# Another order of an attention's instructions, and 91 instead of 58 of its sums on VectorE

## The chip, the core and the metric

The kernel runs on one core of one Trainium2 chip. Its time is the device time of one execution in microseconds (us). In the trace PE is TensorE's matmuls and PEld its weight loads, DVE is VectorE, ACT ScalarE, POOL GpSimd, SP SyncE, which issues most of the DMAs. SBUF is the on-chip memory that all engines share, PSUM the smaller one that matmuls write.

## The reference, cut to what matters

```python
# attention: 4 batches x 8 heads, 1152 keys of 64, queries pooled in pairs (576 of them)
q_pool = q.reshape(B, H, S // 2, 2, D).mean(axis=3)
scores = scale * np.matmul(q_pool, k.transpose(0, 1, 3, 2))
scores = scores - np.max(scores, axis=-1, keepdims=True)
attn = np.exp(scores)
attn = attn / (np.sum(attn, axis=-1, keepdims=True) + 1e-09)
x = np.matmul(attn, v)            # -> 2304 rows x 512
# then a soft mixture of 8 experts (w1, w2) on x, dispatched by softmax over rows of x @ phi,
# and combined by softmax over slots; then
h = x @ w_in
out = (h * np.cos(h)) @ w_out
```

All of it is float32. The weights w_in and w_out are converted inside the kernel, during the attention, into another number format (clamp, shift, sign, round) and stored to DRAM for the last stage.

## The kernel before

The attention works on pairs of heads, p = 0 to 15, and each pair has two halves of the queries, a = 0 and 1, of 288 each. For each half there are nine key tiles, t = 0 to 8, of 128 keys. Per (p, a, t): `scores` (L453) writes a 128 x 576 tile of PSUM with eight matmuls, among them one that subtracts the row maximum; `exps` (L468) on ScalarE takes the exponential into an SBUF tile E, of which there are five; `av` (L493) multiplies by v on TensorE; and `e_sum` (L477) adds E to the running sum ES, also in SBUF. For t = 1 the sum is ES = E0 + E1 (L486), from t = 2 on ES = ES + E (L488), so the sums of one half are a chain. `on_vector` (L474) says whether a sum runs on VectorE or on GpSimd: the table VEC (L48) has one string for each half, and a sum is on VectorE if its t is among the digits.

Before the scores of a pair, `prep` (L880) makes its operands: `sum_q` (L344) adds neighbouring queries (VectorE, SBUF to SBUF), `tr_q` and `tr_k` transpose on TensorE, `q_hi`/`k_hi` and `q_lo`/`k_lo` split the results into two parts on ScalarE and VectorE, and 15 `max_pair` (matmuls, L410) with 15 `max_pair_red` (L420, a maximum on VectorE from PSUM into the tile nm) find the row maxima. These maxima of pair p+1 are spread among the scores of pair p. `fin` (L926) turns the sums into reciprocals and normalises the pair; after every fourth pair it also computes that batch's share of the mixture's dispatch (`b_logits`, which reads phi, and what follows).

`convert(i)` (L959), i = 0 to 31, turns one piece of w_in or w_out: load, two ScalarE steps (`conv_act`, `conv_low`), three VectorE steps in SBUF (`conv_clamp` L296, `conv_shift` L302, `conv_sign` L308), a GpSimd addition (`conv_round` L314) and a store. Conversions are spread over the attention too.

Each of these is an `Op` that `add()` puts on a list, 2,500 in all, with what it depends on. `in_order` (L118) then issues them in the order that ORDER (L54) writes out: two characters are one index into the list, in base 64 by DIGITS. Each engine works through its own instructions in that order and waits by semaphores for what they need; nothing else ties the engines' times to each other. An Op with `take="2"` uses one of four PSUM slots, one with `take="E"` one of the five E tiles; each takes the slot that has been free longest in the list.

SyncE issues the loads and stores in the order of the same list, each of them waiting for its buffer: q, k and v, the conversions, phi, the first 40 pieces of the experts' weights into a ring (`ring_piece`, 256 KB each) and further pieces (`late_piece`) into buffers that the attention has done with. After the attention the mixture's experts consume these pieces while the ring loads the rest; the last stage (cosine and two matrix products) follows.

Of the kernel before, what the change touches and what calls it, by code (L numbers as in the profile page):

```python
# [52 lines left out]
)  # L53
ORDER = (  # L54
    "0102XrXs0304050H0809XuXvXw06070L0M0P240Q0B0C0R0SXtXx0F0G0J220N0K0I0O0D0W0E0T0A0U0V0X0Y230Z28290l0m2B0o0pXy0s000t"
    "0w0x0+0a250-0bXz262C46470q272D0c0d2A0n0r0u0y100v0z1112X+2E0g0h13140e0f0iY017181B1F1C2L2M15191D2F161AY11G1E1IY22G"
# [2 lines left out]
    "2j3037382e2f2m3B3C3F3G6B4N4O2n2o3J3K4VYDYCYEYF4W4XYGYH34393D3H3L3A3E4Y3I3M1y1z3O3N4R3P4S3R3S3V3W4e3Z3d4f3aYI1+4P"
    "4QYL3T3X4T3Q4U3U3Y3c3e3g4Z1-3h4L4a3i3j3m3nYJYK4M3b3f3q3r3u4k483v4b6E4c3l3p4l3t3k3o3s3x8Y6F4d4t6I3w3yYM4g4wbsbtYN"  # L60
    "204u4+4h4x214i4-4jYOYP4yYQYRYS525356576G6H6K6L3z4v4z506M51556C6J8b3+3-595A4o4p5B545F5C6T5G6U5J5K5N4m4n4q6N6O405E"
    "5O5I5M5QYT4r5R584s6V6W6R5D8Z5H5LAc415S5T5V5Z6S5W5a6b6c5d5e5h5P6d5i6e6Z6a5U5Y42YUYWYXYY5X5bYb5c5fYVYZ43Ya5g5k5l6P"
    "6Q6X5m5q5u5n5y6Y6f5r5j5o5s5v5w5z6k6lbu8e8cAf8d8g8f6g6hYc8h5p5t5x5-6m8i8j606x6+6n6yYe5+8k72766-7073776q6r7A7B4445"
    "616263YfYg748p8q6s6tbr6oYdbvYjYh6z787175796pYi7D6i7E7F6j7G8l7J6u7K7N7R8m7C7H7L7O7P8z8+7S8x8yYk7I7M64YmYnYoCg6v6w"
    "7Q7UAd657VYl66YpYq7W7X8-907Z7a7dYr7e8r8s7h7i7l8v8w6798997Ybw7c7b7m7g7k7o7p8n7f8o7q7r7j7n8t8u918a7u7v7y807z819697"
    "9495YsYuYt7s7w7+Ag92937t7x7-839J9M849QAhAk9K9U9N68Yv9A7T9R9VYw82859Y699BAiAmAe869OYxYz879Z9S9CCjAnAoAjAl9L9P9T9X"
    "9Wbx9D9b9c9E9d9F9e9h9iAr9G9l9p8889As9m9a8A8BAt9fAu9q9H9I9g9kYybyY+Z0Y-9o9s9t9u9jAz9n9vA+9x9-9y9zZ1A0AxAyA3A7A1Z2"
    "8CA4B1Ek9w9+A28D8IA8B2Z58JAvAwA6AAZ3Z4AB8MA-8NACB0ADAGApAHbz8K8LAqAKAOA5A9ALB3AEB4AP9rZ6B5Z8Z9Z78O8PChAI8E8F8GCk"
    "EnB6B7AMAQAFAJANZAARZBZDClCoAS8S8T8HBABBBNBOb+BQBRBSBCBDZCBUBVBYB8BZB9BcBd8Q8RCmBWBaBeBIBJCnATCp8UAUAV8VBPBTBXb-"
    "c0BbBfBgZEBGBHBhBlBEBiBmBjZGBpBqBFBKAWAXAYCzC+8WBLBM8XCiBtZHZICxCyc1BnBrBuCtBkBoZFZLCuZJAZBsBwBxZKCqCrByB-C3BvBz"  # L70
    "CsC0C4C-D0C7C8D5D6CBCGH9CCD3D1ZMB+D2ZNC2C6CAc2C1D4CHCECFElZOZPCvCwCKC5C9c3CDCICLCMD7D8D9COCSZQZTZREoCPCQEpDAEsCT"
    "CJCNCRCVCWDBDEDFZSDRDSDCDDDUDVDYDcDZDdDGDHCUDgDhAaAbCXCYCZEqErDWEuEmDKEvHCDLEwDTDXDbc4Etc5ZUZVDfDjDkZWEzE+DlDmDM"
    "DNDpDtDaDqZXDxDuc6CaCbDIZYF3DoDsDJDODwDeDiDnDrCcDPDyD+ZZZaDQE0DvDzF4D-F1CdE3E1ZbE7F2c7E4ExE8EBEFEyECF9FAE-E2E5E9"
    "E6EAEGF7FBF0F8F5ZcEDEEEIF6EJEKHAEOESEHELc8CeFCFDEPJDEMEQETc9CfEUEWEXFIZeHDZfZgZjFEZdHEENFFEREVEZFJHHFGEaFHFVFWFO"
    "FPEYFYFcFZFdFgFhFKFLFkFlFpHFHJHGJGHIFXHKHLFbZhZiZkZlZmcAcBFfFjFnEbFaFeFiFqFoEcZnEdFtFuZoHMFxF-HNFQZpZqFyFMFmFrFs"
    "FRG0FNFSFvFzFwF+G2G3FTHQFUHWHRG4G5HXG7G8cCG9GBGCHUHVGFGGGJZrHYEeHZEfGDHBHOHPJEZsZuG6GAGEZvZwGKGIGMGNGHHcGOZtZxHd"
    "HaGPHbEgGSGWGaGLGTGQHSGXZyHhGbGRGVHTEhcDJHHeHfHgGUHiGZGdGeHwHlJIJLHzHxZzI1G1cEHmH+GYGcI2I5I6HpI9HqEiIAJJEjJNLHJO"
    "JPZ+Z-GfGga0a1JKH-cFa2HyI0I4GhJMI8ICIDHjHkIEIFHnHoIIIJLIIMIQI3I7cGIBJYINJZHrHsHtIHILIRIPITa3GiIUGjHuHvIGJSJWIVGk"
    "GlJTIKIOISIYIcIWJQJXIZIaIdJRIgIeIkIhJUJVJgIiIlImIXIbIfJcJhLKJea5GmGnIjInIoJfJdGoGpa4a6GrJaGqJbIpIqItIuJiIxIyJnJo"
    "I-J0cHGwGxIrJlJmGyGzLLcIJja8JkIvLMLNLOGsGta9a7aALPIsIwcJLQI+NLcKJFJ2J3H0H1GuGvIzJ+J-JpJ1JqK1K5K2LRK6LSLULVJ4J5K9"  # L80
    "LTaDJtJ6KAKDKIaBaCK3JuKEaEK7JvJwLYK0K4LZK8KCaGaHKJaFKGKHNMG+G-aILaLbKMKNKQH2LWKRLXJ7J8KBcLKUaLKFH3JrH5H7JsJxJyH4"
    "KVJzaJKKKOKSaKJ9H6JAH8aMaNKLKPKTNOKXKYKWaOKZKcKaLkaPKdLlKgKhKkKoKeKlLeLfLiLjKbKfKjKnKiKmPmLJKpKrKsKqKtaQKuLgKxLh"
    "KyK-L0LcKvLdLmL3NRL4aRJBJCKzL1NPNSLnNQLoNTKwK+L2NUL6L7LtLuM2M5M3cMM6LpLqaTcNM9MAL5M7NYL8NZL9aSLzMDMHL+aUaWMENVNW"
    "LxaXaYLANXMIM4M8MCMGLyMKaVMLLvMBPpLwMMLrMQMUMNLsMFMJaZLBMRMOMSMVMYNmNeNfcOcPMZMWMPMTMXL-M0M1RqMbNnMcNgNhMdMgMeMh"
    "NcMaaaMiNdLCMkMoMlMpNoNpMsLDMxMtNiNjabacadaeafNaNbMfMjMnLEMrMyMvMwNkNlMmMqM-N0NtNuN3N4PnN7PsNqN8agNvNrNwMuMzN1M+"
    "N2N6NAPtPvahNBNxNsO6NyO7NNLFLGO9OAO1O2ODcQOHaiOENzN5N9NCOIN+NDPwPxajPycRNEOLOMN-O0PqO3PrO8OCPuOGRrOBOFOJakOKOOam"
    "anaoOPRtO4O5OQOUalORP-OVcSONQ0OYOZOcOdPzP+NFarOSapNGNHNIQ5OWQ6OTOXOaObOfOgOhQ1OiOkOoQ2OlQ3aqOpOsOeOwQ4Q9cTQ7OtQA"
    "asauavOjOnawOrOvOxOzO+QBO-atNJQ8QCOmOqP0OuP3TuNKQDPoP7P4QEQFP8PBaxPCazQIQJRwOyRuP1RxRzRvRyQGQHP5P9P2P6PAPEPFaya+"
    "b0QXQaQeQYQbb1QfQiQjb2PDQQQRQcQmQgQkQnQoPGPHPIR+R-S0QMQKRsQLQZQdQhQNTvQlQpQqS1S2Qra-QsQOQPQvQzQwQtQ+PJPKS5PLS6R1"
    "R2b3PMQSQTSFQuQUb5QyR0SGQVR4TxR5QWR6S3R9RDR7QxQ-R3S4SBRARESCRHRIRLS7S8RMPNPOR8RCRGRKb4b6b7RBROPTRPPUS9RQSDPPb8b9"  # L90
    "bAbBbDRFSASERRPQSHPSPRRJRURYSIRcbCRVRZRNPdSJSKRdSLTyRSRWPVPePWSMSNRTRXRbPfTzRfPZSQbEU0bGRgVySbPgbFbHPaSRPXSeScSW"
    "PYbISfSXRaSiSjSmPbSnSOSPRePiPcT+SgPhU2bLPjU3U4bJbKT-PkPlVzRhRiRjU1SqSrSSSTSUSdbMShSlSpStSuSVSkSYSZSvSaSwSoSsSxbO"
    "UBUCSzS+T1T2U5U6T5T6TATBS-U9UAUDRkUESyT0T4T8bPT9TDTET3ULT7UMTHTwRlTLRmTITMTFTJUFTPUHcfRnbQTCTGTQUGUITKTObNbRV-TS"
    "TTU7TUTNU8UJTVTYTcUKUNTZTdchTgUSThUTUQTRTWW0W1UOUPTXTbW4TaTeTiURTfTjTkUYUZUabTbSbUUfUgUiUmUbUjUqUnUrbWbXUWUXUuUv"
    "RoRpbYW2UUbbTlcUTmUhTnUkUoUsUlW3UpUtUVbVUcUxUyW5UdUeUzU+UwWJWKV1V2V5V6WDV9WEVAVEbZbaU-WBWCW9V0V4VFV8V+ToTpVCWAbc"
    "VDbdWFWGW6W7W8VHV3VLVPVTVIV7cgVMWLWHTqbebfbgVJVNbhbiVQVRVGTrbjVKVOVSWIVUVWWMWPVYVcVXWQVZVdWNWOWRVgVhWaVkTsVbVfVj"
    "WbVVVaVeViVlVmVBbkblVnVockWSWTVpVqVrTtWYWZWjWmWkcnbmWUWnWqWVWrbnWuWvWeWfWyboWzcbX1WoWcWdbpVsVtVuWWWXWgWlX2WpWtWx"
    "W-cVVvWscWWwWhWiW+X3cccdX5X0X9X6XAXDX7XBXEX4X8XFXCXGXIXLXHcpVwXJXMVxcZclXPXTXXXQcmcXXKXOcYcqcoXNXRcjcicaXUXYXVXZ"
# [1430 lines left out]
```

## Time and profile before

| | us |
|---|---|
| median of 3 runs | 802.92 (799.06 to 803.47) |
| the profiled execution | 802.07 |
| its span, first to last instruction | 800.3 |
| attention up to the first scores | 24.05 |
| from there to the last pair's first scores | 460.15 |

The page lists for the whole span: PE busy 739.7 us, DVE 603.8, ACT 448.8, POOL 455.3. A busy PE is not PE at its peak, since matmuls overlap and their ends are modelled. Waits are read with the engine that ended them: "A <- B" means that A sat idle until B's instruction was done. A row with three durations gives the shortest, median and longest of a group.

### The profile page before, as it was taken

Reading aid. Unit: us, or ns where it says so; the run is one execution under the profiler, and the core shown is the slowest. Engines: PE = TensorE matmul, PEld = TensorE weight load, DVE = VectorE, ACT = ScalarE, POOL = GpSimd, SP = SyncE. Lnnn points to the kernel's source line nnn. Section 1 sums busy time; section 2 is a strip of 40 time slices with the busy share of each in tenths; the row PEclk is TensorE's granted clock in tenths of the full one; section 3 lists DMA queues with packets and bytes.
Section 4 is the critical chain, followed back from the end, with each engine's and each line's share of the span. In section 5 each row is a group of like instructions: output and inputs, shape, how many; then the busy total and the mean of one; then the engine's idle time right before and its main releaser. Section 6 shows DMA issues by size and latency. Waiting matters only on the chain.

```text
span 800.3 us, 16402 instructions
## 1 busy us (share of the span) xinstructions
PE 739.7 (92%) x6336; PEld 536.9 (67%) x6336; DVE 603.8 (75%) x902; ACT 448.8 (56%) x838; POOL 455.3 (57%) x373
## 2 busy tenths in 40 slices
...
GB/s 228 74 101 106 188 75 180 128 167 133 141 203 116 231 84 145 121 142 191 118 110 127 41 124 162 236 332 384 386 55 26 28 27 20 8 27 27 27 27 26
DMA packets 86482, 101.48 MB, mean 127 GB/s; under 512 B 48260, under 2 KB 48260, under 8 KB 86404
## 3 DMA queue, kind: packets, MB, share of 16 engines
...
q10 hardware_dynamic: 6020, 0.34, 0.5%
...
q14 instruction: 28, 0.23, 0.1%
...
## 4 chain that ended last, share of the span: by engine, by line
PE 59%; DVE 26%; DMA 6%; issue 4%; ACT 3%; POOL 1%; SPq 0%; DVEq 0%; ACTq 0%; POOLq 0%
PE o L1433 15%; PE mx L460 11%; PE mx L498 9%; DVE nm L424 8%; PE o L1435 8%; PE mx L415 4%; PE mx L463 3%; DVE cvt L304 3%; DVE cvt L310 3%; DVE ES L488 3%; DVE cvt L298 2%; PE h L1229 2%; PE u L1397 2%; DVE qs L347 2%; DMA w<-in_moe_w_dram 1%
## 5 line engine op out<-in xcount | busy, mean ns | idle before, releaser
L488 POOL TENSOR_TENSOR ES<-ES,E 128x576 f32<-128x576 f32 x169 | 246.3, 1459 | 65.2 <-DVE ES L488 35.1
L424 DVE TENSOR_REDUCE nm<-mx 128x2 f32<-128x768 f32 x240 | 222.8, 950 | 38.1 <-PE mx L415 37.0
L471 ACT ACTIVATE E<-mx 128x576 f32<-128x576 f32 x288 | 178.2, 651 | 95.3 <-PE mx L463 80.4
L460 PE MATMUL mx<-Q,kX 64*128 64x288 f32 x1152 | 174.8, 318 | 17.3 <-DVE nm L424 13.7
L498 PE MATMUL mx<-E,vn 128*64 128x288 f32 x1152 | 157.6, 416 | 0.0
L1417 POOL TENSOR_TENSOR lo<-g,hi 128x512 fp32r<-128x512 f32 (+1 forms) x73 | 94.2, 1290 | 110.7 <-DVE hi L1415 105.9
L460 PEld LDWEIGHTS mx<-Q,kX 64*128 64x128 f32 x1152 | 113.1, 192 | 38.4 <-DVE nm L424 20.4
L498 PEld LDWEIGHTS mx<-E,vn 128*64 128x64 f32 x1152 | 76.8, 138 | 57.3 <-ACT E L471 6.8
L1433 PE MATMUL o<-w_hi,hi 128*128 128x512 f32 x288 | 113.1, 393 | 0.7 <-DVE hi L1415 0.7
L1435 PE MATMUL o<-w_lo,hi 128*128 128x512 f32 x288 | 113.2, 393 | 0.3 <-DVE w_lo L1321 0.3
L415 PE MATMUL mx<-kX,Q 64*128 64x384 f32 x480 | 88.3, 389 | 17.3 <-DVE nm L424 9.0
L460 PE MATMUL mx<-Q,kY 64*128 64x288 f32 x576 | 88.1, 300 | 0.0
L463 PE MATMUL mx<-NM,one_row 64*128 64x288 f32 x576 | 87.9, 299 | 0.0
L1433 PE MATMUL o<-w_hi,lo 128*128 128x512 f32 x288 | 77.4, 389 | 0.0
L1404 DVE SCALAR_TENSOR_TENSOR r<-t,u 128x512 f32<-128x512 f32 (+1 forms) x73 | 49.4, 678 | 36.5 <-ACT t L1402 35.9
L1413 DVE SCALAR_TENSOR_TENSOR g<-r,u 128x512 f32<-128x512 f32 (+1 forms) x73 | 49.6, 679 | 35.4 <-ACT r L1411 35.3
L1402 ACT ACTIVATE t<-u 128x512 f32<-128x512 f32 (+1 forms) x73 | 42.9, 591 | 58.2 <-PE u L1397 58.1
L415 PEld LDWEIGHTS mx<-kX,Q 64*128 64x128 f32 x480 | 45.9, 193 | 40.8 <-DVE nm L424 17.5
L316 POOL TENSOR_TENSOR cvt<-cvt 128x512 uint32<-128x512 uint32 x32 | 43.2, 1350 | 40.3 <-ACT cvt L294 14.6
L486 POOL TENSOR_TENSOR ES<-E 128x576 f32<-128x576 f32 x28 | 41.8, 1494 | 40.3 <-ACT E L471 34.7
L1433 PEld LDWEIGHTS o<-w_hi,lo 128*128 128x128 f32 x288 | 54.0, 188 | 11.5
L1433 PEld LDWEIGHTS o<-w_hi,hi 128*128 128x128 f32 x288 | 54.2, 188 | 10.8 <-DVE hi L1415 0.9
...
## 6 DMA issues: line engine op xcount, KB each, us to landing
...
```

The source lines that it names most:

```text
L415: nc.tensor.matmul(out=m[:, h, 0:384], lhsT=Q1[p % 2][hs, AT[i]:AT[i] + 128], rhs=X[p][hs, ks], start=True, stop=True)
L424: nc.vector.tensor_reduce(out=nm3[p][:, i, :, c:c + 1], in_=m[:, :, 0:384], axis=AX.X, op=ALU.max)
L460: nc.tensor.matmul(out=sc[:, h, 0:HF], lhsT=x[hs, ks], rhs=y[hs, qs], start=(n == 0), stop=False)
L463: nc.tensor.matmul(out=sc[:, h, 0:HF], lhsT=one_row[hs, :], rhs=NM[p % 2][hs, qs], start=False, stop=True)
L471: nc.scalar.activation(out=e, in_=sc[:, :, 0:HF], func=AF.Exp, scale=1.0 / 16.0)
L488: eng.tensor_tensor(out=ES[p, a], in0=ES[p, a], in1=E[p, a, t], op=ALU.add)
L498: nc.tensor.matmul(out=av_t[p, a, g][64 * h:64 * h + 64, 0:HF], lhsT=vn[p][:, h, t, :], rhs=E[p, a, t][:, h, :], start=(t == g), stop=(t = ...
L1404: nc.vector.scalar_tensor_tensor(out=r, in0=t, scalar=MAGIC, in1=u, op0=ALU.subtract, op1=ALU.subtract)
L1413: nc.vector.scalar_tensor_tensor(out=g, in0=r, scalar=1.0, in1=u, op0=ALU.subtract, op1=ALU.mult)
L1417: nc.gpsimd.tensor_tensor(out=lo[:, 0:n], in0=g, in1=hi[:, 0:n].bitcast(FP32), op=ALU.subtract)
L1433: nc.tensor.matmul(out=o, lhsT=x, rhs=w_hi[ff], start=(ff == 0 and not part), stop=bool(part and ff == NF - 1))
L1435: nc.tensor.matmul(out=o, lhsT=x, rhs=w_lo[ff], start=False, stop=False)
```

## The change

Two tables are replaced: VEC, whose digits go from 58 to 91, and ORDER, the whole list. With them, the load of phi becomes the first Op of the list instead of one after the conversions (so that all indices shift by one), and `b_logits` names it among what it depends on. No instruction's form changes; 33 additions move from GpSimd to VectorE, and all 2,500 Ops are issued in another order.

```diff
 VEC = (
-    "38", "3", "", "27", "2", "4", "", "7",
-    "4", "5", "28", "", "6", "8", "", "458",
-    "", "68", "78", "136", "", "6", "46", "567",
-    "12", "256", "34", "3", "4", "12678", "2345678", "1234567",
+    "468", "1", "45", "2468", "25", "237", "4", "1267",
+    "36", "6", "6", "12367", "68", "67", "15", "7",
+    "568", "1", "4578", "126", "4", "24568", "4", "2367",
+    "234", "17", "238", "137", "67", "123568", "2345678", "1234567",
 )
 ORDER = (
-    "0102XrXs0304050H0809XuXvXw06070L0M0P240Q0B0C0R0SXtXx0F0G0J220N0K0I0O0D0W0E0T0A0U0V0X0Y230Z28290l0m2B0o0pXy0s000t"
...
+    "020304050709060G080H0A0OXsXt0PXu0Q0R0M0N0E0F0C0D0S0I0J0K0L2429010T2A0U0X0Y0V0b0W0m23250B2C0n0p0t0x0qXvXwXxXyXz26"
...
 )
...
-                bl[b] = m = add(b_logits, b, deps=[mul[p], bp0.get(b - 1), bp1.get(b - 1)], take="2")
+                bl[b] = m = add(b_logits, b, deps=[mul[p], bp0.get(b - 1), bp1.get(b - 1), lp], take="2")
...
+        lp = add(load_phi)
         for p in range(NP):
             prep(p)
             main(p)
...
         for i in range(NU):
             convert(i)
-        add(load_phi)
```

Decoded, the beginning of the list reads before: sum_q(0), tr_q(0), conv_load(0), conv_act(0), q_hi(0), tr_k(0, first part), k_hi, max_pair, tr_k (second part), k_hi, conv_clamp(0), conv_shift(0), conv_sign(0), q_lo(0), k_lo(0), and the maxima. After: sum_q(0), tr_q(0), q_hi(0), tr_k, q_lo(0), tr_k, k_hi, max_pair, k_lo, the first maximum, k_hi, max_pair, conv_load(0), conv_act(0), and more maxima; conv_clamp(0), conv_shift(0) and conv_sign(0) come after the first four scores.

## Rows read from the trace of the kernel before

**Rows 1.** Stretches: length; PE, PEld, DVE, ACT, POOL busy us; clock, DMA share, GB/s.
```profile
24.05:484.20 460.15, 424.87 (x4545) 306.41 (x4543) 407.38 (x533) 272.53 (x504) 329.25 (x240) 0.98 0.47 133
484.20:527.30 43.10, 38.64 (x350) 24.78 (x346) 30.32 (x62) 17.61 (x39) 2.87 (x3) 0.96 0.68 215
527.30:575.60 48.30, 46.59 (x351) 19.09 (x352) 13.80 (x58) 16.82 (x48) 13.85 (x33) 1.00 1.04 382
```

**Rows 2.** Who waited for whom, 24.05 to 484.2 us: total us, times, longest us.
```profile
PEld mx L460 <- DVE nm L424: 20.4, 28, 1.9
...
PE mx L460 <- DVE nm L424: 13.7, 14, 1.7
PEld mx L415 <- DVE nm L424: 12.2, 16, 2.1
```

**Rows 3.** Groups, 24.05 to 484.2 us: xcount | busy us, mean ns | idle before, releasers.
```profile
L488 POOL TENSOR_TENSOR ES<-ES,E 128x576 f32<-128x576 f32 x169 | 246.3, 1459 | 65.2 <-DVE ES L488 35.1 <-ACT E L471 14.1 <-DVE ES L486 6.2
...
L488 DVE TENSOR_TENSOR ES<-ES,E 128x576 f32<-128x576 f32 x41 | 36.8, 898 | 2.6 <-POOL ES L488 1.8
L310 DVE SCALAR_TENSOR_TENSOR cvt<-raw,cvt 128x512 uint32<-128x512 uint32 x30 | 32.2, 1072 | 0.7
L304 DVE TENSOR_SCALAR cvt<-cvt 128x512 uint32<-128x512 uint32 x30 | 28.9, 962 | 0.7
L298 DVE TENSOR_SCALAR cvt<-cvt 128x512 f32<-128x512 f32 x30 | 23.0, 766 | 1.4 <-ACT cvt L289 1.3
...
L347 DVE TENSOR_TENSOR qs<-qn 96x768 f32<-96x768 f32 x15 | 21.6, 1437 | 0.0
```

**Rows 4.** Shortest, median, longest ns by tile or line, whole span.
```profile
L488 POOL TENSOR_TENSOR ES<-ES,E x169: 1395/1421/2033, 28.6 to 479.5; 128x576 f32<-128x576 f32 x169
...
L488 DVE TENSOR_TENSOR ES<-ES,E x54: 736/757/1833, 32.1 to 509.2; 128x576 f32<-128x576 f32 x54
...
L298 DVE TENSOR_SCALAR cvt<-cvt x32: 409/476/1677, 10.7 to 485.2; 128x512 f32<-128x512 f32 x32
L304 DVE TENSOR_SCALAR cvt<-cvt x32: 409/879/1661, 11.1 to 486.5; 128x512 uint32<-128x512 uint32 x32
L310 DVE SCALAR_TENSOR_TENSOR cvt<-raw,cvt x32: 674/693/1840, 11.6 to 488.9; 128x512 uint32<-128x512 uint32 x32
...
L347 DVE TENSOR_TENSOR qs<-qn x16: 943/1370/2081, 5.8 to 444.4; 96x768 f32<-96x768 f32 x16
...
L424 DVE TENSOR_REDUCE nm<-mx x240: 889/949/965, 13.7 to 490.5; 128x2 f32<-128x768 f32 x120
```

**Rows 5.** Order of time, about 199 to 203 us: start us, us, engine.
```profile
197.62 5.99 POOL L488 TENSOR_TENSOR ES<-ES,E 128x576 f32<-128x576 f32 x4
...
199.34 1.53 DVE L304 TENSOR_SCALAR cvt<-cvt 128x512 uint32<-128x512 uint32 x1
...
200.79 1.81 DVE L424 TENSOR_REDUCE nm<-mx 128x2 f32<-128x768 f32 x2
...
202.73 1.44 DVE L310 SCALAR_TENSOR_TENSOR cvt<-raw,cvt 128x512 uint32<-128x512 uint32 x1
```

**Rows 6.** The chain that ended last, shares of the span by line.
```profile
by line: PE o L1433 15.1%; PE mx L460 10.5%; PE mx L498 9.4%; DVE nm L424 7.7%; PE o L1435 7.6%; PE mx L415 4.1%; issue 4.0%; PE mx L463 3.0%; DVE cvt L304 2.9%; DVE cvt L310 2.7%; DVE ES L488 2.7%; DVE cvt L298 2.2%; PE h L1229 1.8%; PE u 
```

**Rows 7.** Order of time, the kernel's first 22 us.
```profile
6.90 1.19 PE L358 MATMUL mx<-idn,qs 96*128 96x96 f32 x6 [6.90 <-DVE qs L347]
8.32 0.90 PE L382 MATMUL mx<-idn,kn 64*128 64x64 f32 x12 [0.22 <-DMA kn<-in_k_dram]
9.98 0.66 ACT L289 ACTIVATE cvt<-raw 128x512 f32<-128x512 f32 x1 [7.97 <-DMA raw<-in_moe_w_in_dram]
...
11.07 0.81 ACT L397 ACTIVATE kX<-mx 128x768 fp32r<-128x768 f32 x1
...
12.88 0.95 DVE L401 TENSOR_TENSOR kY<-mx,kX 128x768 fp32r<-128x768 f32 x1
...
13.75 7.99 DVE L424 TENSOR_REDUCE nm<-mx 128x2 f32<-128x768 f32 x9
```

More of the change, by code (lines that the diff above doesn't have):

```diff
@@ L48 @@
 VEC = (
[4 rows of a table removed]
[4 rows of a table added]
 )
 ORDER = (
-    "0102XrXs0304050H0809XuXvXw06070L0M0P240Q0B0C0R0SXtXx0F0G0J220N0K0I0O0D0W0E0T0A0U0V0X0Y230Z28290l0m2B0o0pXy0s000t"
-    "0w0x0+0a250-0bXz262C46470q272D0c0d2A0n0r0u0y100v0z1112X+2E0g0h13140e0f0iY017181B1F1C2L2M15191D2F161AY11G1E1IY22G"
-    "0j2R0k2VX-1J1K2S1L1N1R1V2W1HY31O1P2N1S1W2O1T1Z1e49Y41a2H2T2U1X1M1Q1U1f2I1Y1c1d2J2K1i1j1m1n2P2Q2X1q1r2a2b4C4D4A4F"
-    "1b1g4B4E2Y1k2ZY5Y6Y81h1l1p1t1u2c2d1o4G4H4I2p2s2q2t2w2x4J4K2+322-1s2gY9YA6A6D2k1v2u33Y72r2v2z312h1w1x2l2y3536YB2i"
@@ L59 @@
[L59 to L98, printed above, removed]
@@ L99 @@
-    "XSXWXaXbXcXdXgXkXpcrcsXhXlXqctXfXjXnXoc+XeXiXmc-d0bqcecwcucvcyd1d2cxczd3"
+    "020304050709060G080H0A0OXsXt0PXu0Q0R0M0N0E0F0C0D0S0I0J0K0L2429010T2A0U0X0Y0V0b0W0m23250B2C0n0p0t0x0qXvXwXxXyXz26"
+    "0u0-0y0c100h0i0o0s0w2D0Z0a0d2E0r0+12132F0e27X+2814150v0z2B1118191C1D160f0g1G1H2W0j2XX-Y1Y21A17Y01B1F1J0k0l2M1K2N"
+    "2G1L1O1M1P1S1W1a2H1E1I2I1T2UY31X1Q1U474A1N1R1V1Z1b2V1d1e2J2O2PY41f1g2S2T1j1k1n1o2Q2R1Y1r1s2K1i2L1c482Y4D4E4H4I1h"
+    "1l2b2c4JY64G1m1q4BY5Y74C2Z2a1u1v1p4F6C2j2k2q2r2t2u2l2m2x2y2-2h306B2i1t1wY81x334WY94K1y4X002s2w2+32YAYB4L3436372v"
@@ new lines @@
+    "2z2f2g2d383C393G3KYC2e2n3D31353H1z4f3A4S3B3E3L2obs6E2p3F3J1+YE1-YD4g3N3P3O4T4OYF3Q3S3W3a3I4P3T3XYHYI3b4Q4RYJ3e3U"
+    "3Y4Y4Z4a3R3V3Z3dYG8Z3f3hYK203i3c4bYM4U4V3j3k3n3o3M4M3r3s3v4N4c6F3w3g6G6J4d3m3l3q3uYL3yYNYPYO4h49YQ4e3p3t3z4i4u4v"
+    "4j4k4x4-534y4z503x544l4m57213+58226H6L3-YRYUbt514n4w4+6I6K6M6N52565A5B40YSYT4o55595C4p5D5G5K4q5O4r5H6O6a5L5P8c5E"
+    "8a5F4s4tAd5J5N5R6b6UYVYW6P5I5M5SYX6V5T5W5U5XYY5a5b5e6S5YYZ5i5f416W6c6T6X5VYa6d5Z425d5hYb5j5lYc43446Y5m5c5g5kbu5n"
+    "5r6Z5o5p5s6Q6R5v5Q5w6e6f5z5+6g6D6lbv6m8f8g8iYdYf8d6h6i8eYe5q5u5t5x5y60616y5-8q8h6z8r6-737071776pYgYhYi747B787C6q"
@@ new lines @@
+    "45468b6263648j8kAg6jYk8l6+72767A7E7F6k756n6o7G8m7H7K7L7O8n7S7P797D7T6r6s6tYjYl7J6u7N7R6v7V6wbwChbx7I6x8oAe8+7M65"
+    "7W7Q667X7a8p7Y7e7i7b8-YnYoYp7m907f7c7j67997Z7d687g7n7k7oYs919AYm7h7l7p7q8w8x7r7sby8y8z7v7z7w817+8s8t8uYqYr7u8v7y"
+    "8082AhAi9293947t7x7-83Al84857U9798YtYv9K9L9N9O9PAf696AYu9R9VYw9S9W9B9C9Z9aYxY+8687Aj88An95969M9QAk9TAmAo9UAp9Y9c"
+    "9d9X9F9G9e9f9D9E9HYy9i9m9j9b9n898A9q9rCkA+A-8B8CYzAsAt9h9l9I9JY-Z09p9t9g9k9o9vZ1Z29u9w9yAu9zA09sA4A1bzAvA5A8Z3Z6"
+    "A9B2B3AwAx9x9-9+8D8EZ4Ayb+AzZ5b-A3A7ABAC8J8KB0B18NA28OA6AAADAEAHAIAqArElALAPAMAQ8P8QB4B5B68FClAFZ78GAJAN8IB7CmCp"
@@ new lines @@
+    "Z9ZAB8AGAKAOASZ88H8T8LAT8UBBZBZCBO8MBCCiBPBJBKBRBSBVZDBZBWBaBDBE8VAR8WAUAV8RZE8SB9BABdBeBHAWBTBic0c1BICnBFBXBGCo"
+    "ZFZGCqZHZIZJBQBUBLBYBcBjBbBfBgBhCrBmBqBuZKCsCtBkBnZMBrCuC+CvBlc2C-BpBtBvZLBxByBMD6AXBoBsBwEoCyBNAYAZD78X8YBzCzB+"
+    "C0C4C1D4C5D5C8C2C9CCCHCDC6CAD0CwCxEmZNB-C3C7CID1CBCFCGD8ZOD9CLCMD2CPCQCTD3EpDADBCECJCNHAAaZPZQCKCOCSZRZSDCCUCjCR"
+    "CVEqEtCWCXDSc3DTc4DDDVDEHDDWDXDZDaDdDFZTDeDhAbCYDGDiErZUAcDHCZCaDbDfc5DjEnEvDUDIDYDcEwExDgDJEsZVEuDKDmDnDLDMc6Dk"
+    "Dlc7DNZWDOCbZXDoDqDrDPDuJEDyDvDzCcZYCdZZZaE+E-F4F5CeDpDsDtDxD-DQDRE0F0F1F2E1E2E4F3E5DwD+E6E8ECE9EDEyEzZcEGEHELF6"
```

26 lines of the change are left out of this document (added).

## Prediction

> **What bounds the kernel now.** I read the stretches first [rows 1]. The attention's steady part runs from the first score matmul at 24.05 us to the last pair's at 484.2 us, 460.15 us long. In it VectorE is busy for 407.38 us and TensorE for 424.87 us; ScalarE (272.53 us) and GpSimd (329.25 us) have room. TensorE's time has holes, and the waits say who makes them: three rows in which matmuls or weight loads wait for VectorE's row maxima (nm, L424) come to 20.4 + 13.7 + 12.2 = 46.3 us [rows 2]. A maximum is late because something stands ahead of it in VectorE's queue. So VectorE decides.
>
> Then the groups in that stretch against the shortest instance of each line. The reader is to see that five groups on VectorE are much longer on average than at their shortest [rows 3, 4]: clamp L298 766 against 409 ns (x30: 10.7 us over), shift L304 962 against 409 (16.6), sign L310 1072 against 674 (11.9), the q sum L347 1437 against 943 (x15: 7.4), the sums L488 898 against 736 (x41: 6.6). Together 53.2 us of the 407.38 are stall, not work. What these five have in common is that both operands, or source and result, lie in SBUF. The maxima read PSUM, and theirs stay within 889 to 965 ns [rows 4]. The order of time shows the stall itself: GpSimd runs four sums without a pause from 197.62 to 203.61 us, L304 starts at 199.34 and needs 1.53 us, L310 starts at 202.73 and needs 1.44 us; two maxima stand between them in VectorE's queue and come that much later [rows 5]. L304's longest instance, 1661 ns, is its shortest plus 1252 ns, which is within one GpSimd sum (1395 ns at its shortest) [rows 4]. A VectorE instruction of this kind seems to wait until GpSimd's running one is over. GpSimd loses less: its sums average 1459 ns, 64 ns over the shortest, 10.8 us in 169 [rows 3, 4].
>
> How much of a VectorE microsecond reaches the end: the chain that ended last holds 2.9 + 2.7 + 2.2 = 7.8% of the span on L304, L310 and L298, 62.4 us of 800.3 [rows 6]. These lines are busy 28.9 + 32.2 + 23.0 = 84.1 us in the stretch, about 88 with the two conversions outside it [rows 3], so 0.71 of their time lies on the path. I take 0.71 for every gain or loss of VectorE in this stretch.
>
> **The change part by part.**
>
> *33 sums from GpSimd to VectorE.* The digits in VEC go from 58 to 91. A sum on VectorE takes 757 ns (median, [rows 4]): +25.0 us on VectorE. GpSimd loses 33 x 1421 ns = 46.9 us; it was not the bound, so that alone gains nothing.
>
> *The order.* Decoding both lists, I count for each of VectorE's SBUF instructions (sums, clamps, shifts, signs, q sums) whether the next GpSimd instruction in the list still waits for something that comes later in it, so that it can't run into this one. That holds for 69 of 170 before and 127 of 203 after. Of the 91 sums, 39 follow a GpSimd sum that they wait for, against 23 of 58, and such hand-overs can't collide with the one before them. So the list does what it says, in part: 101 instructions were open before, 76 are now, which would scale the 53.2 us to 40; GpSimd also holds the port 46.9 us less of its 329.25, which makes it 34. The count doesn't see where GpSimd stands in time when VectorE comes, only what may overlap. The ends are 0 (all kept apart) and 58.5 us (nothing gained, and the 33 new sums stall by L488's 162 ns each, 5.3 us). I take 22 us, two thirds of the way from 0 to the 34 that the counts alone give. It is nearer to the counts because the timing in the list is a plan, and a GpSimd sum (1421 ns) drifts across a 409 ns shift easily. VectorE then has 25.0 - (53.2 - 22) = -6.2 us, times 0.71: **-4.4 us**. By both ends: -28.2 x 0.71 = -20.0, and +30.3 x 0.71 = +21.5.
>
> *The head.* Before, the first conversion's ScalarE step stands ahead of q_hi in ScalarE's queue and waits for its load: it starts at 9.98 us and lasts 0.66, though the q transposes are done at 6.90 + 1.19 = 8.09; q_hi comes after it, then kX at 11.07, and VectorE does clamp, shift and sign (0.41 + 0.41 + 0.67 us at their shortest) before the first maximum at 13.75 [rows 4, 7]. In the new list q_hi comes first and the conversion's VectorE part after the first scores. q_hi can start at 8.1, kX when the k transposes end at 8.32 + 0.90 = 9.22, and the first maximum at about 11.0 (kX 0.81, the low half kY 0.95): 2.7 us earlier, with the same nine maxima ahead of the first row. The 1.5 us of conversion fall due later, in a pair whose VectorE work grows. Between 1.2 and 2.7, I take **-2 us**.
>
> *The tail.* Twelve quarter-megabyte weight pieces now stand behind the last scores in SyncE's queue (three before). From 484.2 to 527.3 us the DMA engines are busy 0.68 of the time, 13.8 us are free; twelve pieces at the 382 GB/s of the next stretch are 8.2 us, so they fit, mostly [rows 1]. From 527.3 to 575.6 us the engines are full (1.04), so what is late is paid. Between 0 and 8.2, I take **+1 us**, because other pieces have moved forward. Of the other moves on SyncE's queue, the small load of phi now comes at the 22nd score instead of the 58th, and the wait added to b_logits is for a load some 67 scores back: nothing, and if the queue's order delays a k or q load, the price is in the upper end of the range.
>
> Sum: 802.07 us of the profiled execution - 4.4 - 2 + 1 = 796.7, that is 797. The median of the runs shown is 802.92, 0.85 us above that execution; a version unchanged would be expected between the two.
>
> **The rivals.**
>
> *Slower: VectorE takes on 25 us and the stalls hardly fall.* If what counts is only how long GpSimd occupies the port, the stalls go from 53.2 to 53.2 x (329.25 - 46.9) / 329.25 = 45.6 us; VectorE gains 17.4 us of work, times 0.71 is +12.4, with head and tail +11: 813 us. It decides from 28.2 us of remaining stall on, where VectorE's account is even. For it: three of the five stalled groups belong to the conversion, whose 96 instructions are all still there, and GpSimd's next instruction after 40 of their places (and after 10 of the 16 q sums) is free to start. Against it: the share of open places falls for every kind but the q sums. The Trainium skill, "SBUF — State Buffer", section "SBUF: two separate sides", says that a VectorE instruction with two SBUF inputs or in a two-port mode and a GpSimd one hold a shared pair of ports exclusively, for the whole instruction, and the other waits; the trace agrees (1661 ns against 409), and by that rule alone, with the order left out, this rival's 813 us would be the result.
>
> *No change: hand-overs take the gain.* 39 sums wait for GpSimd ahead of the maxima in VectorE's queue, 16 more than before, and every maximum behind one waits with it. A GpSimd sum lasts 1421 ns; if each new hand-over holds VectorE for a quarter of that, 16 x 0.36 = 5.7 us, the account is even: 802 us. For it: VectorE is never far from GpSimd in the new list. Against it: before, with 23 of them, VectorE's sums waited 1.8 us for GpSimd's in the whole stretch [rows 3].
>
> *A large gain: kept apart almost wholly.* With 5 us of stall left VectorE has 23.2 us less, times 0.71 is -16.5, and with the whole 2.7 us of the head and nothing in the tail it gives 783 us. For it: 46.3 us of TensorE's waits are there to be won. Against it: the counts above.
>
> **How the numbers follow.** The forecast has 0.42, with an own range of 791 to 802; slower 0.23, no change 0.21, large gain 0.14. What a measurement of this kernel can tell from no change is about 0.5%, 4 us on either side of 802.9. Below 798.9 lie 0.8 of the forecast, the whole large gain and a little of the no-change case: 0.34 + 0.14 + 0.03 = 0.51. Above 806.9 lies nearly all of the slower case and a rest of the third: 0.23. 0.26 stays within. The range reaches from the large gain (783, a microsecond under) to the slower case's middle (812): about 0.2 is left outside, most of it above.
>
> **What the profile after would show.** Right: L298, L304 and L310 near their shortest on average (under 0.55, 0.6 and 0.8 us), the five groups' excess near 22 us in the attention, 91 sums on VectorE near 760 ns, VectorE's busy time in the attention some 6 us lower, TensorE's waits for nm below 46 us, the first score matmul near 21.5 us, and the full DMA stretch as long as before. Wrong: an excess of 40 us or more (the slower rival), a row of VectorE waiting for GpSimd's sums of 5 us and more (the hand-overs), or less VectorE time with the same TensorE gaps, in which case 0.71 fails.

## The result and the profile after

The changed kernel takes **775.52 us** (median of 4, 774.19 to 778.18); the kernel before, run beside it on the same chip, 803.19 (799.06 to 803.66). The ratio is 0.967 [0.963, 0.971]. The forecast was 797 with a range of 782 to 812: the direction was right, and the gain of 27.7 us is over four times the 6 us forecast, outside the range.

The profiled execution of the changed kernel took 778.18 us, its slowest of the four (span 776.4; before 802.07, span 800.3). The stretches, with the columns of [rows 1]; the attention's steady part comes first, the full-DMA stretch last:

```profile
20.60:457.10 436.50, 419.80 (x4539) 300.12 (x4537) 393.70 (x569) 270.68 (x502) 284.03 (x208) 1.00 0.52 145
...
503.50:551.50 48.00, 46.39 (x343) 18.81 (x336) 13.94 (x57) 16.78 (x48) 13.74 (x33) 1.00 1.04 376
```

The first score matmul starts 3.45 us earlier (24.05 to 20.60), the steady part is 23.65 us shorter, and from the last pair's first matmul to the end it takes 319.3 us instead of 316.1. The start and the end nearly cancel, so the steady part is the matter. In it TensorE's idle time (length less busy time) falls from 35.3 to 16.7 us, its busy time by 5.1 us. VectorE does 33 more sums (27 of L488, six of L486) and is busy 13.68 us less; GpSimd is busy 45.22 us less; TensorE's granted clock shows 1.00 where it was 0.98. The full-DMA stretch is as long as before.

The groups in the steady part (busy us, mean ns), against [rows 3]:

```profile
L488 POOL TENSOR_TENSOR ES<-ES,E 128x576 f32<-128x576 f32 x142 | 208.2, 1467 | 94.5 <-DVE ES L488 66.6 <-ACT E L471 15.2 <-DVE ES L486 5.2
...
L488 DVE TENSOR_TENSOR ES<-ES,E 128x576 f32<-128x576 f32 x68 | 51.7, 760 | 1.9 <-POOL ES L488 0.5
...
L310 DVE SCALAR_TENSOR_TENSOR cvt<-raw,cvt 128x512 uint32<-128x512 uint32 x31 | 23.1, 747 | 0.7
...
L304 DVE TENSOR_SCALAR cvt<-cvt 128x512 uint32<-128x512 uint32 x31 | 19.6, 633 | 0.7
L298 DVE TENSOR_SCALAR cvt<-cvt 128x512 f32<-128x512 f32 x32 | 18.6, 580 | 0.2
...
L347 DVE TENSOR_TENSOR qs<-qn 96x768 f32<-96x768 f32 x15 | 16.2, 1082 | 0.0
```

Each of the five VectorE groups is nearer its shortest instance: the shift L304 averages 633 ns where it took 962, the q sum L347 1082 where it took 1437, the sums L488 760 where they took 898. Counted as before (mean less the shortest of the kernel before, times the number, from unrounded durations and with VectorE's sums of L486 among the sums), the five hold 19.1 us of stall against 53.4 (the prediction said 53.2). The shift's row by tile says the same by its median, 427 ns against 879 [rows 4]:

```profile
L304 DVE TENSOR_SCALAR cvt<-cvt x32: 409/427/1642, 21.6 to 458.3; 128x512 uint32<-128x512 uint32 x32
```

Its longest is still 1642 ns: five of the 32 still last over 1500 ns, each of them started while a GpSimd sum was running.

How such a stall ends can be read off each instance. The longest shift of the kernel before and the sum that it met (start us, us):

```profile
116.44 1.41 POOL L488 TENSOR_TENSOR ES<-ES,E 128x576 f32<-128x576 f32 x1
116.47 1.66 DVE L304 TENSOR_SCALAR cvt<-cvt 128x512 uint32<-128x512 uint32 x1
```

The shift starts 0.03 us behind the sum and ends 0.28 us after it. In the kernel before 64 VectorE instructions of the five groups last over 150 ns longer than the shortest, in the changed kernel 24. Every one of these 88 started while a GpSimd instruction was running, and ended at a fixed distance behind that one's end: clamps and shifts 0.28 to 0.29 us, signs 0.55 to 0.56, sums 0.61 to 0.62, q sums 0.81 to 0.82. So semaphores are not all that ties the engines' times to each other, as the description of the kernel has it; this is a second tie.

Who waited for whom in the steady part, against [rows 2]:

```profile
POOL ES L488 <- DVE ES L488: 66.6, 28, 7.5
...
POOL cvt L316 <- DVE cvt L310: 28.7, 7, 19.0
...
PEld mx L460 <- DVE nm L424: 11.5, 24, 1.8
PEld mx L415 <- DVE nm L424: 7.4, 12, 1.6
...
PE mx L460 <- DVE nm L424: 4.7, 8, 1.3
...
DVE ES L488 <- POOL ES L488: 0.5, 2, 0.3
```

The three rows of TensorE waiting for the maxima fall from 46.3 to 23.6 us, by 22.7. That is near the 23.65 us that the stretch lost, but these rows are a choice, and the waits of matmuls and of weight loads can overlap: all rows in which TensorE waits for a maximum fall from 59.3 to 42.2 us. The hand-overs now go the other way: GpSimd waits 66.6 us for VectorE's sums (35.1 before [rows 3]), VectorE only 0.5 us for GpSimd's.

The chain that ended last can't be set against [rows 6] as it stands: followed back from the end, it breaks off in the changed kernel at 297 us, while in the kernel before it reaches the start. For the last 159 us ahead of the last pair's scores both have it, the kernel before (325 to 484.2 us) first, the changed one (298 to 457.1) second:

```profile
by line: PE mx L498 17.8%; PE mx L460 17.2%; DVE nm L424 13.5%; PE mx L415 7.3%; issue 5.3%; PE mx L463 4.9%; DVE cvt L304 4.4%; DVE cvt L310 4.0%; DVE ES L488 3.8%; DVE cvt L298 3.6%; DMA lw<-in_moe_w_dram 2.7%; DVE qs L347 2.4%; DVE kY L4
...
by line: PE mx L498 24.8%; PE mx L460 14.6%; DVE nm L424 11.9%; PE mx L415 8.0%; issue 4.3%; PE mx L463 4.3%; DVE ES L488 3.8%; POOL ES L488 2.7%; ACT E L471 2.6%; PE mx L442 2.2%; DVE cvt L304 1.8%; DVE cvt L310 1.7%; PE mx L523 1.6%; PE m
```

L304, L310 and L298 fall from 12.0% of these stretches to 4.4% (0.9% for L298, beyond the end of the line shown), and the maxima from 13.5% to 11.9%.

### The profile page after: what moved, and what is told of

Same layout as the page of the kernel before. It is cut to its first block, busy times and chain, and to the rows that moved or that the text cites. A ratio compares the mean times of both kernels' runs of the same rounds, so it can differ in the third digit from the quotient of the medians.

```text
span 776.4 us, 16372 instructions
## 1 busy us (share of the span) xinstructions
PE 737.1 (95%) x6336; PEld 532.1 (69%) x6336; DVE 587.7 (76%) x935; ACT 448.9 (58%) x838; POOL 409.5 (53%) x340
## 4 chain that ended last, share of the span: by engine, by line
PE 48%; DVE 9%; ACT 2%; issue 2%; POOL 1%; ACTq 0%; DVEq 0%; POOLq 0%
PE o L1433 16%; PE o L1435 8%; PE mx L498 6%; PE mx L460 4%; DVE nm L424 2%; PE po L1262 2%; PE u L1397 2%; PE h L1229 2%; PE mx L415 2%; DVE ES L488 1%; PE mx L463 1%; PE pm L1341 1%; POOL ES L488 1%; ACT E L471 1%; PE mx L442 0%
## 5 line engine op out<-in xcount | busy, mean ns | idle before, releaser
L488 POOL TENSOR_TENSOR ES<-ES,E 128x576 f32<-128x576 f32 x142 | 208.2, 1467 | 94.5 <-DVE ES L488 66.6
L424 DVE TENSOR_REDUCE nm<-mx 128x2 f32<-128x768 f32 x240 | 221.3, 950 | 26.7 <-PE mx L415 25.8
L460 PE MATMUL mx<-Q,kX 64*128 64x288 f32 x1152 | 171.5, 314 | 9.9 <-DVE nm L424 4.7
L460 PEld LDWEIGHTS mx<-Q,kX 64*128 64x128 f32 x1152 | 111.8, 190 | 30.3 <-DVE nm L424 11.5
L415 PE MATMUL mx<-kX,Q 64*128 64x384 f32 x480 | 87.6, 387 | 5.7 <-DVE nm L424 4.7
L460 PE MATMUL mx<-Q,kY 64*128 64x288 f32 x576 | 87.2, 297 | 0.0
L316 POOL TENSOR_TENSOR cvt<-cvt 128x512 uint32<-128x512 uint32 x32 | 43.4, 1357 | 61.9 <-DVE cvt L310 28.7
L415 PEld LDWEIGHTS mx<-kX,Q 64*128 64x128 f32 x480 | 44.9, 190 | 28.6 <-DVE nm L424 10.9
L488 DVE TENSOR_TENSOR ES<-ES,E 128x576 f32<-128x576 f32 x81 | 61.5, 759 | 2.8 <-POOL ES L488 0.5
```

The source lines that it names most:

```text
L415: nc.tensor.matmul(out=m[:, h, 0:384], lhsT=Q1[p % 2][hs, AT[i]:AT[i] + 128], rhs=X[p][hs, ks], start=True, stop=True)
L424: nc.vector.tensor_reduce(out=nm3[p][:, i, :, c:c + 1], in_=m[:, :, 0:384], axis=AX.X, op=ALU.max)
L460: nc.tensor.matmul(out=sc[:, h, 0:HF], lhsT=x[hs, ks], rhs=y[hs, qs], start=(n == 0), stop=False)
L488: eng.tensor_tensor(out=ES[p, a], in0=ES[p, a], in1=E[p, a, t], op=ALU.add)
```

## The experiments

The changed kernel differs in two things that could each be the cause: the list (ORDER) and the table (VEC). The theory to test: VectorE's stalls behind GpSimd's sums are the whole matter, and they cost more of the kernel's time than 0.71. The rivals: the smaller load of GpSimd does it by itself; the list is better for reasons that have nothing to do with the port (head, tail, balance). "The port" is short for what makes a VectorE step in SBUF wait for a running GpSimd instruction; the expectations call the theory S and the rivals V and L. All times are medians, and each ratio is to the kernel before, run beside it (801.26 to 801.36 us).

**The new list with the old table.**

```
 VEC = (
-    "468", "1", "45", "2468", "25", "237", "4", "1267",
+    "38", "3", "", "27", "2", "4", "", "7",
...
```

> The new list with the old table: 58 sums on VectorE, 33 back on GpSimd. Theory S (the time follows VectorE's account, work plus stalls): VectorE loses 25 us of sums and its stalls rise from about 22 to about 45 us, so the account is nearly even: 772 to 782 us. Theory V (the gain is GpSimd's relief): most of the gain goes, 790 to 803 us. Theory L (the list is the better one in its matmuls and maxima, whoever adds): 770 to 778 us with stalls risen all the same.

801.95 us (10 executions), ratio 1.001 [0.999, 1.002]: the list alone gives nothing. S and L miss; the time lies in V's range, whose mechanism the next run refutes. Its steady part, as a stretch:

```profile
20.60:481.70 461.10, 427.60 (x4539) 300.17 (x4537) 392.56 (x536) 269.98 (x502) 331.75 (x241) 0.99 0.50 138
```

Two of the waits in it:

```profile
DVE ES L488 <- POOL ES L488: 11.1, 7, 3.0
ACT E L471 <- POOL ES L488: 10.5, 10, 2.4
```

And the group of the shifts:

```profile
L304 DVE TENSOR_SCALAR cvt<-cvt 128x512 uint32<-128x512 uint32 x31 | 25.0, 806 | 0.7
```

With the 33 sums back on GpSimd the shift is stalled again (806 ns), the five groups hold 37.9 us, VectorE waits 11.1 us for GpSimd's sums (1.8 before), and ScalarE's exponentials wait 10.5 (2.4 before). That GpSimd runs later than the list supposes would explain all three, and is argued.

**The old list with the new table**, the same lines of VEC the other way round.

> The old list with the new table: 91 sums on VectorE. Theory S: +25 us of work, stalls 53 us before and 45 to 53 now, of which 0.7 to 1 reaches the end: 810 to 828 us. Theory V: 775 to 790 us. Theory L: 803 to 828 us, as S.

848.11 us, ratio 1.058 [1.054, 1.062]: the moved sums alone cost 47 us, more than any of the three ranges had. The steady part:

```profile
24.00:530.80 506.80, 441.33 (x4543) 315.01 (x4543) 420.44 (x566) 275.02 (x504) 279.92 (x207) 0.95 0.43 122
```

And its waits:

```profile
POOL ES L488 <- DVE ES L488: 101.2, 32, 8.1
...
PEld mx L460 <- DVE nm L424: 24.5, 28, 3.1
...
DVE ES L488 <- POOL ES L488: 17.9, 10, 3.1
...
ACT E L471 <- POOL ES L488: 10.1, 12, 2.7
```

VectorE is busy only 13.06 us more than before (420.44 against 407.38), and the stretch is 46.65 us longer. The stall is not what grew: the five groups hold 41.6 us, less than before. The rest is waiting: VectorE for GpSimd's sums 17.9 us, GpSimd for VectorE's 101.2, and a granted clock of 0.95, that is, about a tenth of the stretch at 1.2 GHz. That GpSimd has less to do is thus no gain by itself, and the rival that says so falls.

**The kernel before without the port's load.** GpSimd's sums from the third exponential tile on run over 8 of the 576 columns; the rest of these sums is left out, and every instruction, wait and place in the list stays.

```
-            eng.tensor_tensor(out=ES[p, a], in0=ES[p, a], in1=E[p, a, t], op=ALU.add)
+            n = HF if eng is nc.vector else 4
+            eng.tensor_tensor(out=ES[p, a][:, :, 0:n], in0=ES[p, a][:, :, 0:n], in1=E[p, a, t][:, :, 0:n], op=ALU.add)
```

> The kernel before, with GpSimd's sums from t = 2 on over 8 of the 576 columns only (the rest of those sums is left out), so that GpSimd hardly holds the port. Theory S: VectorE's stalls fall from 53 to about 12 us and 0.7 to 1 of that is gained: 762 to 774 us. Theory L: the old list's own order of matmuls and maxima keeps it above 785 us though the stalls are gone.

757.91 us, ratio 0.945 [0.942, 0.948]. The steady part:

```profile
23.90:440.70 416.80, 409.42 (x4545) 299.64 (x4543) 364.76 (x533) 270.96 (x504) 121.49 (x240) 1.00 0.52 146
```

The shifts in it as a group (busy us, mean ns):

```profile
L304 DVE TENSOR_SCALAR cvt<-cvt 128x512 uint32<-128x512 uint32 x30 | 14.4, 478 | 0.7
```

And GpSimd's sums by tile (shortest, median, longest ns):

```profile
L489 POOL TENSOR_TENSOR ES<-ES,E x169: 193/200/911, 28.5 to 435.5; 128x8 f32<-128x8 f32 x169
```

A GpSimd sum takes 200 ns at the median, and the shift falls from 962 to 478 ns though nothing of VectorE's was touched. The five groups hold 10.7 us of stall, 42.7 less (the three longest shifts left, 906 to 1657 ns, each met a sum for t = 1, which the cut leaves whole); the kernel is 43.4 us shorter, under S's range, which put 0.7 to 1 on each microsecond of stall. A microsecond of stall is worth a microsecond of the kernel here. The Trainium skill, "SBUF — State Buffer", section "SBUF: two separate sides", says that VectorE with two SBUF inputs (or in a two-port mode) and GpSimd hold a shared pair of ports exclusively, each for its whole instruction; the shift's fall to 478 ns agrees.

**The same cut in the changed kernel.**

> The changed kernel with GpSimd's sums from t = 2 on over 8 of the 576 columns only (the rest left out). Theory S: stalls from about 22 to about 5 us, 760 to 766 us, which is no better than the kernel before cut in the same way, since VectorE has 25 us more to add. Theory L: 765 to 772 us and at least 15 us less than the kernel before cut in the same way.

767.37 us, ratio 0.957 [0.954, 0.961]; 8.2 us under the changed kernel's 775.52 (7.9 by the ratios), where the stall falls from 19.1 to 8.0 us. The time lies a little above S's range and in L's, whose other condition fails. The steady part:

```profile
20.60:445.90 425.30, 415.60 (x4539) 298.42 (x4537) 382.68 (x569) 269.59 (x502) 108.48 (x208) 1.00 0.53 148
```

By the medians that is 0.74 us for each microsecond of stall. The profiled executions give 1.0 (a stretch 11.2 us shorter for 11.1 us), but they are the slowest execution of the changed kernel and the fastest of this one. And without the port's load the changed kernel is slower than the kernel before, 767.4 against 757.9.

**The two missing corners of this square**: the cut kernel before with the new table, and the cut new list with the old table (the edits are those above, put together).

> The kernel before with GpSimd's sums over 8 of 576 columns (the rest left out) and the new table, so the 33 sums are added on VectorE with hardly a port to wait for. If an added sum costs what the lists have idle on VectorE, about 0.35 of its time as between the two narrow kernels: 757.9 + 9, 764 to 770 us. If the new list made room for them and the old one has none: 757.9 + 20 to 45, 778 to 803 us.

For the first, 795.36 us, ratio 0.993 [0.989, 0.996]. The steady part:

```profile
23.70:476.60 452.90, 423.68 (x4545) 304.44 (x4543) 388.81 (x566) 271.86 (x504) 107.18 (x207) 0.98 0.47 134
```

Two of its waits:

```profile
PEld mx L460 <- DVE nm L424: 15.3, 26, 2.6
PEld mx L415 <- DVE nm L424: 11.8, 19, 2.5
```

> The changed kernel with GpSimd's sums over 8 of 576 columns (the rest left out) and the old table: the new list without port waits and without the 33 added sums. If the new list made room for the sums and they fill time VectorE would else wait in: at most 9 us below the narrow kernel with the new table (767.4), 758 to 767 us, level with the old list cut in the same way (757.9). If the new list is better in its matmuls and maxima as well: below 755 us. If each added sum costs its full time: 767.4 - 25, 742 us.

For the second, 768.39 us, ratio 0.959 [0.957, 0.962]. The steady part:

```profile
20.70:447.50 426.80, 416.67 (x4539) 297.99 (x4537) 364.68 (x536) 268.87 (x502) 124.05 (x241) 1.00 0.54 148
```

Here the price of the 33 sums stands by itself, with hardly a port in the way. In the old list VectorE's busy time rises from 364.76 to 388.81 us and the stretch by 36.1 (416.80 to 452.90): more than the work itself, since the weight loads of L460 and L415 now wait 27.1 us for maxima (4.7 and 7.7 in the first cut kernel) and the clock falls to 0.98. In the new list VectorE's busy time rises from 364.68 to 382.68, and the stretch doesn't grow (426.80, 425.30): the sums fill gaps left for them. The first run lies in the range for an old list without room, the second 1.4 us above the range for sums that fill idle time. The square in full, with the stall that the cut takes away in the five groups:

| list, table | whole sums, us | cut sums, us | what GpSimd's whole sums cost, us | stall taken away, us |
|---|---|---|---|---|
| old, old (before) | 801.3 | 757.9 | 43 | 42.7 |
| old, new | 848.1 | 795.4 | 53 | 29.7 |
| new, old | 802.0 | 768.4 | 34 | 26.7 |
| new, new (after) | 775.5 | 767.4 | 8 | 11.1 |

In the two crossed kernels whole sums cost more than the stall. There the cut also takes away waits for GpSimd's sums: VectorE's fall from 17.9 to 2.2 us and from 11.1 to 0.8, ScalarE's from 10.1 to 3.1 and from 10.5 to 5.3.

Followed through the square: the cost of GpSimd's whole sums falls by 35.2 us (43.4 to 8.2), the new list is 10.5 us worse without them (768.4 against 757.9), and the moved sums change nothing there (-1.0): a gain of 25.7 us, the difference of 801.3 and 775.5. Taken the other way round, the moved sums cost 37.5 us in the old list and the new list gives 28.0 back; only their total, 9.5 us, does not depend on the way.

**The kernel before with the new head alone** (the first conversion's load and ScalarE step behind the second maximum, its VectorE steps behind the first five scores).

```
-    "0102XrXs0304050H0809XuXvXw06070L0M0P240Q0B0C0R0SXtXx0F0G
+    "01020304050H080906070L0M0P240Q0BXrXs0C0R0SXt0F0G
...
```

> The kernel before with the new head alone: q_hi ahead of the first conversion in ScalarE's queue, the conversion's VectorE steps behind the first four scores. If the head is worth what the first score matmul moved (24.05 to 20.6 us) all of it reaches the end: 3 to 3.5 us less. If the moved conversion only falls due later: 0.5 to 2 us less.

801.91 us (12 executions) against 801.36 (18), ratio 1.000 [0.998, 1.003]. The first score matmul comes at 21.6 us, 2.4 earlier, and the stretch behind it is 3.6 us longer: in the profiled execution the head gives back what it wins. By the interval it is worth 1.6 us at most. That refutes the 3 to 3.5 us; the 0.5 to 2 us expected for a conversion that only falls due later are missed by the medians, and not excluded.

**Improving the changed kernel.** In its tail a small TensorE product (run_col) and VectorE's copy of it (run_put, L761) stand in the list behind four VectorE sums, and a matmul waits for the copy. VectorE in order of time (start us, us):

```profile
468.58 3.33 DVE L488 TENSOR_TENSOR ES<-ES,E 128x576 f32<-128x576 f32 x4
...
471.83 0.14 DVE L761 COPY nM<-mx 32x1 f32<-32x1 f32 x1
```

And TensorE, with the wait ahead of the matmul in brackets:

```profile
472.02 0.40 PE L460 MATMUL mx<-Q,kX 64*128 64x288 f32 x2 [2.26 <-DVE nM L761]
```

So the two go ahead of the four sums (ORDER, decoded):

```
-    e_sum(15,0,5), e_sum(15,0,6), e_sum(15,0,7), e_sum(15,0,8), run_col, run_put
+    run_col, run_put, e_sum(15,0,5), e_sum(15,0,6), e_sum(15,0,7), e_sum(15,0,8)
```

> The changed kernel with run_col and run_put ahead of the last pair's four sums of its first half, where the next score matmul waits 2.26 us for run_put in the trace after. If that wait is on the path: 2 to 4 us less than the changed kernel, so 771 to 774 us beside 775.5. If the sums behind it are on the path as well: 0 to 1 us less.

773.23 us, ratio 0.966 [0.964, 0.969]. VectorE's copy now stands ahead of the sums:

```profile
464.90 0.14 DVE L761 COPY nM<-mx 32x1 f32<-32x1 f32 x1
...
464.97 3.32 DVE L488 TENSOR_TENSOR ES<-ES,E 128x576 f32<-128x576 f32 x4
```

By the medians that is 2.3 us under the changed kernel, by the ratios (0.9671 and 0.9664, each with its own runs of before) 0.6 us, and the intervals overlap: a gain of the wait's size is not shown. For it speaks that from the last pair's first matmul to the end the profiled execution takes 317.0 us instead of 319.3. Its steady part, whose list is that of the changed kernel, shows how far one execution differs from another (433.0 us here, 436.5 there):

```profile
20.50:453.50 433.00, 417.57 (x4541) 297.83 (x4539) 394.59 (x569) 270.31 (x502) 284.07 (x208) 1.00 0.52 146
```

Then, on top of it, seven VectorE steps that the changed kernel's trace shows stalled, each put one place later, behind a step that stood after it (four times a maximum):

```
+    max_pair_red(2,0,2), conv_clamp(2)        +    max_pair_red(2,0,1), conv_shift(3)
+    max_pair_red(3,0,1), conv_clamp(5)        +    k_lo(4,1), sum_q(5)
+    pair_mul(2), conv_clamp(8)                +    av_out(4,0,8), conv_shift(9)
+    max_pair_red(8,0,2), conv_shift(16)
```

> The changed kernel with the tail edit, and with seven of the VectorE steps that still stalled in its trace by 0.7 to 1.2 us put one place later, behind a maximum or a PSUM step that was free. Theory S: those seven lose most of their 7 us of stall, which passes to the end at about 1: 4 to 7 us below the tail edit alone. Rival: the plan is stiff, the moved steps meet GpSimd's next sum instead, 0 to 2 us either way.

771.20 us, ratio 0.964 [0.961, 0.966], the fastest of the kernels that compute everything. The steady part:

```profile
20.70:450.90 430.20, 418.15 (x4539) 298.95 (x4537) 389.55 (x569) 270.25 (x502) 284.91 (x208) 1.00 0.52 147
```

And two groups in it (busy us, mean ns):

```profile
L304 DVE TENSOR_SCALAR cvt<-cvt 128x512 uint32<-128x512 uint32 x31 | 16.8, 543 | 0.7
L298 DVE TENSOR_SCALAR cvt<-cvt 128x512 f32<-128x512 f32 x32 | 16.2, 505 | 0.2
```

The shift falls from 633 to 543 ns, the clamp from 580 to 505, the stall in the five groups from 19.1 to 14.8 us (20.1 with the tail edit alone). The kernel is clearly faster than the one before; against the changed kernel (4.3 us less by the medians, 2.6 by the ratios) the intervals overlap, so that step is likely, not shown. Against the tail edit alone it is 2.0 us, not the 4 to 7 that theory S expected for its stall, about the rival's 2.

Eight more steps (two clamps, two shifts, a sign, two q sums and a sum) moved one or two places later on top, by the stalls in the new trace:

```
+    e_sum(2,1,7), conv_clamp(6)               +    max_pair_red(12,4,2), conv_shift(25), conv_sign(25)
+    max_pair_red(7,0,0), e_sum(6,0,8)         +    max_pair_red(6,4,0), sum_q(8)
+    max_pair_red(14,2,0), sum_q(15)           +    max_pair_red(14,2,1), conv_clamp(29)
+    max_pair_red(4,4,1), conv_shift(8)
```

> The kernel with the tail edit and the seven moves, with eight more of the steps that still stalled by 0.35 to 1.3 us in its trace put one or two places later. If stalls saved by hand keep passing on: 2 to 4 us below 771.2. If the moved steps meet other sums by now: 770 to 773 us.

772.63 us, ratio 0.964 [0.962, 0.967]: no further gain is seen. The five groups' stall went down to 12.6 us, but the stretch was 434.0 us (430.2 before these moves). That difference is about what one execution differs from another, so what 2.2 us less stall is worth here can't be told.

## Why the prediction was wrong

**The size of the stalls was right.** 22 us were forecast to stay and 19.1 did. The reading behind it (both operands in SBUF, the wait at most one GpSimd sum long, the maxima untouched) was shown twice: each stalled instruction ends at its fixed distance behind the GpSimd instruction that it met, and with GpSimd's sums cut the same instructions at the same places lose 42.7 us. Of the signs named for the profile after, clamp and shift stayed above theirs (580 and 633 ns, named under 550 and 600). That 22 came so near is in part luck: it was two thirds of a count that says what may overlap, not what does.

**The 25.0 us for 33 sums were right as work.** 760 ns each. VectorE's busy time fell by 13.7 us instead of 6.2: 8.2 of it are the five groups with their new sums, 1.5 the maxima, 1.9 two groups of small steps (L694, L703), and the rest was not followed up; 0.71 of 13.7 would still be only 9.7 us.

**The step that failed is the 0.71 for every gain or loss of VectorE.** It was read from the share of three lines on the chain that ended last, and put on stalls and sums alike. The runs give two different prices:

- Stall in the kernel before passes on whole: 42.7 us of it are worth 43.4 us. By the intervals that is 0.96 to 1.09 for each, where 0.71 was put. In the changed kernel 11.1 us are worth 8.2 by the medians, and the intervals allow 0.3 to 1.1 for each, so that 0.71 and 1 can't be told apart there. That the chain's share was too low for the kernel before, from which it was read, is understandable (a chain shows one path, and a stalled conversion that isn't on it pushes back the maximum behind it all the same), but this reason is argued, not shown.
- Added work passes on by where the list puts it: the same 33 sums cost 37.5 us in the old list (757.9 to 795.4, cut sums) and nothing in the new (768.4, 767.4), where 0.71 of their 25.0 us had put 17.8. The prediction had the list as a means to keep two engines apart, and missed that it also puts the sums where VectorE is idle.

Term by term, through the square: the sums were put at +17.8 us and came to -1.0; the stall was put at -22.2 (31.2 us less of it, at 0.71), and GpSimd's whole sums, with the stall down by 34.3 us, cost 35.2 us less; the new list by itself is 10.5 us slower, for which the prediction had no term. That is 18.8 + 13.0 - 10.5 = 21.3 us more gain than the 4.4 forecast, the 25.7 us of the square. So the largest part of the miss is the price of the added sums, and two errors were partly paid back by a third. Which of the new list's many places make it slower was not tried.

**The clock is part of it, and by how much is only estimated.** From [rows 1] and the same row after, 17.1 us of the steady part were at 1.2 GHz and 3.4 are now (twice the part of the clock that is missing, times the length, from unrounded clocks). Over 18 executions of the kernel before, from 796.99 us at a mean clock of 0.993 to 805.07 at 0.985, a line gives 0.38 us of the kernel per microsecond at the lower level. By that 13.7 us less would be, as an estimate, some 5 of the 24. The clock does not go with the stalls as such: with the sums cut none of the stretch is at 1.2 GHz in the old list with the old table (10.7 us of stall), but 17.1 us with the new table (11.9). In these two TensorE sits idle for 7.4 and 29.2 us of the stretch. No run separated the clock from the rest.

**The head** came 3.45 us earlier (2 forecast), but the kernel before with the new head shows no gain: the 1.5 us of conversion that fall due later were priced only in the lower end of the range (1.2 us), and the stretch behind the new head gave back all of it. **The tail** cost 3.2 us (1 forecast), not for the weight pieces, since the full stretch is as long as before, but up to 2.26 us of it for a copy behind four sums, which the prediction did not look at.

**The rivals.** The large gain came closest (783 forecast for 5 us of stall); it was priced with the same 0.71 and so took 5 us of stall for a gain that came with 19.1. The slower one's mechanism, that the stalls follow only GpSimd's load, is refuted for this change: at nearly the same load (331.75 and 329.25 us) the new list with the old table holds 37.9 us of stall and the old list 53.4. Within the old list it comes near: at 279.92 us of load its rule gives 45.4 us, and 41.6 were measured. The hand-overs did not appear in the changed kernel (0.5 us), but they are real where list and table don't match: 11.1 and 17.9 us.

**What stays open.** In the cut kernels GpSimd also finishes its sums earlier, which might help whoever waits for them. Against that as the cause in the kernel before: VectorE waited 1.8 us for GpSimd's sums there [rows 3] and ScalarE's exponentials 2.4, and the 43.4 us agree with the stall taken away. In the crossed kernels these waits were larger, and there the price of the stall alone stays open. It was not tried separately.
